# First MLP layer of chunks 2 to 5 by seven products over both halves, with staging in the MLP's tile and unpadded keys

## The chip, the cores and the metric

The kernel runs on one core of one Trainium2 chip. The metric is the device time of one execution in microseconds; for each kernel the median of several runs is given. Everything is computed in 32-bit floating point.

## The reference, cut to what matters

A delta-rule attention over B = 4 batches, H = 8 heads, S = 768 tokens and D = 48, followed by an MLP over all 3072 tokens, which see the eight heads side by side (384 features):

```
k_n = k / (norm(k) + 1e-6)
for t in range(S):
    y[t]  = q[t] @ state
    v_old = k_n[t] @ state
    state = state + beta[t] * outer(k_n[t], v[t] - v_old)
x = y, tokens in rows, 384 features
h = x @ w_in              # 384 -> 2048
out = (h * sigmoid(h)) @ w_out   # 2048 -> 384
```

## The kernel before, in words

The attention is computed in six chunks (NCH) of 128 tokens (C), each in two halves of 64 (W). All 32 pairs of batch and head go together, in two groups g of two batches. Within a half, the recurrence is solved with the inverse of a triangular 64x64 matrix per head. For a chunk c the steps are:

- **Scores** (`prepare`, `score`, line 550). Keys and queries are needed with D on the partitions. For chunks 0, 1 and the keys of 2 `turn` (line 514) transposes them on TensorE, with four 128x128 transposes into one bank. From then on `load_blocks` (line 151) fetches them by DMA in blocks of 32 into `stage`, and `turn_blocks` (line 504) transposes these on VectorE (DVE) with the 32x32 stream transpose of line 509. The products of keys with keys and queries leave PSUM through ScalarE and through `mask` on DVE (line 560). `block_out` and `block_in` send the key blocks through DRAM into another layout, g ("g<-blocks").
- **Inverse** (`invert`). 31 steps of a rank-one update on DVE, each a pair of operations (lines 648 and 653), and a last one (656); a copy of g (568); the results go through DRAM again ("low", "up", "xe").
- **Solve** (`solve`), a generator of nine steps: `merge` (801) twice, `keys` (843: state times keys, and the subtraction from v at line 852), `inner` (854, evacuated as z), `old` (923), `update` (872: the products pu, and their addition to the state at line 886) and `new` (935). The output of the attention, `pyc`, becomes `xT`, the transposed input of the MLP, by copies and DMAs.

The MLP of chunk c has two halves of 256 tokens. `hidden(c, hf)` (line 1061) makes w_in products: for each of 8 f, two j and three blocks a of 128 input features one matmul 128x128x256, 48 for a half; each float32 matmul is two instructions in the trace. A Silu on ScalarE (1078) puts 128x512 into `gT`, a tile out of a pool of three. `combine(c, hf)` then does the second layer by seven products instead of eight of block matrices (line 1175, chains of eight matmuls with 192 columns), with sums of g made on DVE by `sum_g` (1157) and sums of w_out made once.

The order of every engine's instructions is written out by hand (`pin`). For chunks 0 and 1 a script text gives it; from the end of chunk 1 a loop does. The MLP of the chunk before is cut into pieces by `yield`; `run(n)` puts n pieces at that place in the order of TensorE (and of the engines that evacuate). So the MLP's pieces lie between the steps of the attention. A piece of `hidden` is three or so matmuls, one of `combine` four. Almost all DMAs are issued from SP's queue, one after another in program order.

Where the loop of chunk c stood, before: nine steps of solve(c) with pieces between them, two steps of prepare(c + 1) with two pieces each, the scores, eight pieces, the 31 steps of the inversion with three pieces to four steps, and ten pieces with the squares and norms of chunk c + 2's keys (`lengths`).

## Time and profile before

| | us |
|---|---|
| median of three runs | 638.84 (637.5 to 639.85) |
| span of the profiled execution | 643.2 |
| busy in it: TensorE (PE) | 626.0 |
| VectorE (DVE) | 398.6 |
| ScalarE (ACT) | 216.7 |
| GpSimd (POOL) | 93.7 |

The profile is of one execution and is a little longer than the median of the runs. PE is TensorE's matmul unit, PEld its load of weights, which lies beside matmuls. An engine's busy time over the span says how much of the time it worked, not whether something waited for it; that is read from the chain of work that ended last, from timelines and from windows of the trace. Durations of single matmuls in the groups are latencies and overlap; the rate is read from stretches of the chain.

### The profile page before, as it was taken

How to read it: one execution, taken by the hardware profiler on the slowest of the kernel's cores; microseconds unless marked ns; L12 is line 12 of the kernel's file. 1: busy time of each engine (PE TensorE's matmuls, PEld its weight loads, DVE VectorE, ACT ScalarE, POOL GpSimd, SP SyncE). 2: the span in 40 equal slices, each digit the busy share in tenths (PEclk: the TensorE clock that was granted, in tenths of full speed). 3: DMA queues.
4: the chain of work that ended last, by engine and by line, in shares of the span. 5: the costliest groups of instructions: out<-in, count | busy, mean ns of one | idle time of the engine just before them, and what ended most of it. 6: DMA issues, size and time to landing. Idle time of an engine off the chain costs nothing.

```text
span 643.2 us, 21887 instructions
## 1 busy us (share of the span) xinstructions
PE 626.0 (97%) x9650; PEld 550.3 (86%) x9650; DVE 398.6 (62%) x902; ACT 216.7 (34%) x510; POOL 93.7 (15%) x95
## 2 busy tenths in 40 slices
PE   7889999999999999999999999999999999999997
PEld 5677778666689988999989999989989989889997
DVE  5853788998765985563986563987565974212112
ACT  3554756142342122452122451122451122441120
POOL 5422721246010020010020010020001000000000
PEclk9858999999999999999999999999999999999999
DMA  7755554170369333368433268334173033100101
GB/s 153 176 111 175 189 117 112 50 148 4 85 129 153 56 90 38 61 131 143 57 87 47 52 132 145 63 83 52 36 146 75 12 78 46 40 14 1 25 0 25
DMA packets 141694, 53.68 MB, mean 83 GB/s; under 512 B 113296, under 2 KB 135056, under 8 KB 141600
## 3 DMA queue, kind: packets, MB, share of 16 engines
q1 hardware_dynamic: 141120, 51.62, 39.6%
q8 instruction: 76, 1.25, 0.9%
q10 hardware_dynamic: 480, 0.67, 0.4%
q14 instruction: 18, 0.15, 0.1%
HBM read 39.62 MB, written 10.49 MB: 78 GB/s over the span
## 4 chain that ended last, share of the span: by engine, by line
PE 94%; DVE 3%; issue 2%; DMA 1%; SPq 0%; ACT 0%; POOL 0%; DVEq 0%; POOLq 0%
PE phid L1068 40%; PE px L1175 16%; PE py L1175 12%; PE po L1103 7%; PE pa L550 3%; PE pz L859 2%; PE ph L847 2%; PE pyc L940 2%; PE pu L879 2%; PE pyc L927 1%; PE pt L521 1%; PE px L801 1%; PE py L801 1%; PE pw L349 1%; PE pl L752 1%
## 5 line engine op out<-in xcount | busy, mean ns | idle before, releaser
L1068 PE MATMUL phid<-xT,w_in 128*128 128x256 f32 x1152 | 259.4, 383 | 0.2
L1068 PEld LDWEIGHTS phid<-xT,w_in 128*128 128x128 f32 x1152 | 216.8, 191 | 31.7 <-issue 2.1
L1078 ACT ACTIVATE gT<-phid 128x512 f32<-128x512 f32 x88 | 52.5, 597 | 146.0 <-PE phid L1068 138.8
L648 DVE SCALAR_TENSOR_TENSOR rank<-g,step,x 128x31 f32<-128x31 f32 (+15 forms) x124 | 49.8, 401 | 37.4 <-DMA g<-blocks 34.0
L1157 DVE TENSOR_TENSOR sums_of_g<-gT 128x384 f32<-128x384 f32 (+1 forms) x60 | 30.6, 530 | 55.4 <-ACT gT L1078 44.8
L1175 PE MATMUL py<-w_out,sums_of_g 128*128 128x192 f32 x320 | 56.8, 329 | 0.0
L1175 PE MATMUL px<-sums_of_w,sums_of_g 128*128 128x192 f32 x320 | 56.6, 329 | 0.0
L1175 PEld LDWEIGHTS px<-sums_of_w,sums_of_g 128*128 128x128 f32 x320 | 52.2, 190 | 0.5
L1175 PEld LDWEIGHTS py<-w_out,sums_of_g 128*128 128x128 f32 x320 | 52.2, 190 | 0.4
L653 DVE TENSOR_TENSOR x<-x,rank 128x31 f32<-128x31 f32 (+15 forms) x124 | 42.5, 343 | 4.3
L488 POOL TENSOR_TENSOR vf<-vf,n_slot 128x768 f32<-128x768 f32 x10 | 14.7, 1478 | 168.2 <-DMA vf<-in_v_dram 93.0
L886 DVE TENSOR_TENSOR state<-state,pu 48x384 f32<-48x384 f32 x44 | 24.3, 552 | 23.2 <-PE pu L879 22.3
L565 ACT COPY xT<-pyc 48x128 f32<-48x128 f32 (+2 forms) x120 | 31.1, 259 | 1.6
L509 DVE STREAM_TRANSPOSE kq<-stage 128x512 f32<-128x512 f32 x28 | 28.0, 1101 | 3.6 <-DMA stage<-in_q_dram 3.1
L1175 PE MATMUL px<-sums_of_w,gT 128*128 128x192 f32 x160 | 28.4, 329 | 0.0
L1175 PE MATMUL py<-w_out,gT 128*128 128x192 f32 x160 | 28.4, 329 | 0.0
L1175 PE MATMUL px<-w_out,gT 128*128 128x192 f32 x160 | 28.0, 327 | 0.0
L859 PEld LDWEIGHTS pz<-vf,xi 64*64 64x64 f32 x768 | 25.1, 142 | 3.2 <-issue 2.6
L571 POOL COPY g<-x 64x256 f32<-64x256 f32 x4 | 5.0, 1242 | 155.4 <-DVE x L656 155.4
L1175 PEld LDWEIGHTS px<-w_out,gT 128*128 128x128 f32 x160 | 26.4, 190 | 0.5
L859 PE MATMUL pz<-vf,xi 64*64 64x48 f32 x768 | 26.7, 226 | 0.0
L1175 PEld LDWEIGHTS py<-w_out,gT 128*128 128x128 f32 x160 | 26.1, 190 | 0.3
(202 smaller groups left out, 833.7 us busy)
## 6 DMA issues: line engine op xcount, KB each, us to landing
vf<-in_v_dram SPq DMA_DIRECT2D x48, 96.0 KB, 3.3
out_dram<-o SPq DMA_DIRECT2D x42, 96.0 KB, 2.2
w_out<-in_moe_w_in_dram SPq DMA_DIRECT2D x12, 256.0 KB, 3.3
sums_of_w<-in_moe_w_out_dram SPq DMA_DIRECT2D x8, 384.0 KB, 3.9
blocks<-ap SPq DMA_DIRECT2D x40, 64.0 KB, 1.9
kb<-in_k_dram SPq DMA_DIRECT2D x12, 192.0 KB, 4.4
kb<-in_k_dram SPq DMA_DIRECT2D x24, 96.0 KB, 4.5
raw<-in_moe_w_in_dram SPq DMA_DIRECT2D x9, 256.0 KB, 3.8
```

Of the source, the lines that this page charges most:

```text
L509: pin(nc.vector.transpose(out=kqs[c, b][:, :, j, :].rearrange("p a (i m) -> p a m i", i=T), in_=src.rearrange("p a (m d) -> p a m d", d=D) ...
L550: pin(nc.tensor.matmul(pa[e][half, p * n * W : (p + 1) * n * W], lhsT=kq[rows, p, 0, half], rhs=kq[rows, p, js[0] : js[-1] + 1, half], sta ...
L565: return pin(nc.scalar.copy(to, of))
L648: pin(nc.vector.scalar_tensor_tensor(out=tv, in0=g[:, 0:m, m : m + 1].to_broadcast([P, m, n]), scalar=step[:, m : m + 1], in1=x[:, m : m + ...
L653: yield pin(nc.vector.tensor_tensor(out=x[:, 0:m, m:T], in0=x[:, 0:m, m:T], in1=tv, op=ALU.add))
L859: yield pin(nc.tensor.matmul(pz[rows, n * D : (n + 1) * D], lhsT=xis[g][rows, u * H + 2 * p + e, :], rhs=vfs[c][rows, hf, g * HB + u, p, : ...
L886: pin(nc.vector.tensor_tensor(out=to, in0=to, in1=by_heads(pu[of]), op=ALU.add))
L1068: pin(nc.tensor.matmul(ph[:, j * GT : (j + 1) * GT], lhsT=w_in[:, a, (2 * f + j) * P : (2 * f + j + 1) * P], rhs=xTs[c, hf][:, a, :], star ...
L1078: pin(nc.scalar.activation(out=hidden_of(c, hf, f), in_=ph[:], func=ACTF.Silu, scale=-0.5 if in_blocks(c) else 0.5))
L1103: pin(nc.tensor.matmul(pos[i][:, 0:DM], lhsT=hidden_of(0, hf, f // 2)[:, at : at + C], rhs=w_outs[f // HFF][:, f % HFF, :], start=(f == 0) ...
L1157: pin(nc.vector.tensor_tensor(out=sums_of_g[:, k, fs], in0=of[0], in1=of[1], op=op))
L1175: pin(nc.tensor.matmul(to, lhsT=at, rhs=quarter(f, *b) if isinstance(b, tuple) else sums_of_w[b][:, f], start=start and f == 0, stop=f == ...
```

## The change

- **Hidden layer by products of blocks.** For chunks 2 to 5 `hidden_by_products` takes both halves, `early` and `late`, together. Two of the three input blocks (a = 0 and 1), the two halves of the tokens and the two column sets j make a 2x2 by 2x2 product of blocks, computed by seven products; the third block stays plain. Per chunk these are 44 items of two matmuls of 128x128x256. Needed for it: sums of w_in in `wS` (`sum_w_in`, eight operations on DVE, once), differences of x per chunk (`sum_x`, five on DVE), and parts that are put into gT by ScalarE (`keep`) and added to there from PSUM by DVE (`add`, 12 of 128x512 per chunk). It takes one bank from each of the pools A and CC and two of pool M during its 44 items.
- **Staging.** `stage` is gone; the blocks of k and q are loaded into parts of gT (one constant tile now), of `ap0s` (single now) and of wS. Keys, z and queries lie unpadded, so that `turn` uses eight matmuls of 128x64 by the identity in place of four transposes.
- **Order.** The loads of q group 0 stand after the first merge, those of group 1 behind the transposes of k's group 0; q's transposes stand in the solve, ahead of `made` (update and new) of the second half. The scores of c + 1 follow the solve after one piece; the loads of v follow the round trip of the blocks; the inversion has one piece with each step. A cycle consumes 72 pieces where it was some 60. `combine` goes over f in another order and keeps one `kept` part.

The diff, cut to its core:

```diff
...
-    kbufs = [const.tile([P, B, NP, 2, W], FP32, name=f"kb{s}") for s in range(2)]
-    zbuf = const.tile([P, B, 2, NP, W], FP32, name="z")
+    ROW = HB * H * D
+    PADDED = ROW + W - D
+    kbufs = [const.tile([P, 2, PADDED], FP32, name=f"kb{s}") for s in range(2)]
+    zbuf = const.tile([P, 2, PADDED], FP32, name="z")
...
+    gT = const.tile([P, 2, NFF // 2, 2 * GT], FP32, name="gT")
+    wS = const.tile([P, 3, NFF // 2, C], FP32, name="sums_of_w_in")
+    halves = [gT[:, i].rearrange("p f t -> p (f t)") for i in range(2)]
+    spare_s = wS[:].rearrange("p k f t -> p (k f t)")
+    ap0s = const.tile([P, 2, HB, H, W], FP32, name="ap0")
+    runs = {}
+    def run_room(c, j):
+        half = halves[int(c == 3)]
+        for g in range(2):
+            at = 0
+            if c == 2:
+                of, at = spare_s, HB * NP * RUN * g
+            elif j == 0:
+                of, at = half, HB * NP * RUN * g
+            else:
+                of = ap0s[:].rearrange("p g u h t -> p (g u h t)") if g == 0 else half
+            runs[c, j, g] = of[:, at : at + HB * NP * RUN].rearrange("p (n r) -> p n r", r=RUN)
...
-        src, kq = (kbufs[c % 2], queries[c] if c < 2 else None)[j][:, b], kqs[c, b]
+        src, kq = (kbufs[c % 2], queries[c] if c < 2 else None)[j], kqs[c, b]
         pt = bank(room, "pt")
         for p in range(NP):
-            pin(nc.tensor.transpose(
-                pt[:, p * C : (p + 1) * C], src[:, p].rearrange("p e w -> p (e w)"), ident[:]
-            ))
+            for e in range(2):
+                pin(nc.tensor.matmul(
+                    pt[W * e : W * (e + 1), p * C : (p + 1) * C], lhsT=wide(src, b, p, e), rhs=ident[:],
+                    start=True, stop=True,
+                ))
...
-                aps[c, g][j] = work.tile([P, HB, H, W], FP32, name=f"ap{j}", tag=f"ap{j}", bufs=2)
+                aps[c, g][j] = ap0s[:, g] if j == 0 else work.tile([P, HB, H, W], FP32, name="ap1", tag="ap1", bufs=2)
...
-            load_blocks(q, c + 1, slice(HB * g, HB * (g + 1)))
+            if c == 1 or g == 1:
+                load_blocks(q, c + 1, slice(HB * g, HB * (g + 1)))
...
+        if c > 1 and in_blocks(c + 1):
+            load_blocks(q, c + 1, slice(0, HB))
...
-            if hf == 1:
-                if c == 1:
-                    follow(c)
+            if hf == 1 and c == 1:
+                follow(c)
                 load_v(c + 1)
+            elif hf == 1 and in_blocks(c + 1):
+                for b in range(B):
+                    turn_blocks(c + 1, b, 1)
...
+    sums_of_x = sums_of_g[:, 0].rearrange("p f t -> p (f t)").rearrange("p (i t) -> p i t", t=GT)
+    def w_of(a, j):
+        return w_in[:, a].rearrange("p (f j t) -> p f j t", j=2, t=P)[:, :, j]
+    def sum_w_in():
+        n = NFF // 4
+        for to, left, right, op in (
+            (wS[:, 0], w_of(0, 1), w_of(1, 1), ALU.add), (wS[:, 1], wS[:, 0], w_of(0, 0), ALU.subtract),
+            (wS[:, 2], w_of(1, 0), wS[:, 1], ALU.subtract), (w_of(0, 1), w_of(0, 0), w_of(0, 1), ALU.subtract),
+        ):
+            for i in range(2):
+                fs = slice(n * i, n * (i + 1))
+                yield pin(nc.vector.tensor_tensor(out=to[:, fs], in0=left[:, fs], in1=right[:, fs], op=op))
+    UNITS = (3, 0, 1, 2)
+    def sum_x(c):
+        early, late = (xTs[c, hf] for hf in range(2))
+        for to, left, right in (
+            (sums_of_x[:, 0], late[:, 0], early[:, 0]), (sums_of_x[:, 1], late[:, 1], sums_of_x[:, 0]),
+            (late[:, 0], late[:, 1], late[:, 0]), (sums_of_x[:, 2], early[:, 1], sums_of_x[:, 1]),
+            (sums_of_x[:, 3], early[:, 2], late[:, 2]),
+        ):
+            pin(nc.vector.tensor_tensor(out=to, in0=left, in1=right, op=ALU.subtract))
+    def hidden_by_products(c):
+        rooms = [A.popleft(), CC.popleft()]
+        held = [bank(M, "hu") for _ in range(2)]
+        outer = [banks.tile([P, 512], FP32, name="hx", tag=tag) for tag in rooms]
+        early, late = (xTs[c, hf] for hf in range(2))
+        scale = -0.5
+        def product(to, weights, moving, fs, start=False):
+            for i, f in enumerate(fs):
+                pin(nc.tensor.matmul(
+                    to[:, GT * i : GT * (i + 1)], lhsT=weights[:, f], rhs=moving,
+                    start=start and i == 0, stop=True, skip_group_check=True,
+                ))
+        def at(fs, j, hf):
+            return gT[:, hf, fs[0] : fs[0] + 2, GT * j : GT * (j + 1)]
+        def of(held):
+            return held[:].rearrange("p (f t) -> p f t", f=2)
+        def keep(room, fs, j, hf):
+            return lambda: by_act(at(fs, j, hf), of(room))
+        def add(room, fs, j, hf):
+            return lambda: pin(nc.vector.tensor_tensor(
+                out=at(fs, j, hf), in0=at(fs, j, hf), in1=of(room), op=ALU.add
+            ))
+        def silu(fs, j, hf, room=None):
+            to = at(fs, j, hf)
+            return lambda: pin(nc.scalar.activation(
+                out=to, in_=to if room is None else of(room), func=ACTF.Silu, scale=scale
+            ))
+        def both(fs):
+            to = gT[:, 1, fs[0] : fs[0] + 2, :]
+            return lambda: pin(nc.scalar.activation(out=to, in_=to, func=ACTF.Silu, scale=scale))
+        items = []
+        for k in range(2):
+            a, b = ((2 * u, 2 * u + 1) for u in UNITS[2 * k : 2 * k + 2])
+            ua, ub = held
+            xa, xb = outer
+            items += [
+                (xa, w_of(1, 0), early[:, 1], a, True, None),
+                (ua, w_of(0, 0), early[:, 0], a, True, keep(ua, a, 0, 0)),
+                (xa, w_of(2, 0), early[:, 2], a, False, add(xa, a, 0, 0)),
+                (xb, w_of(1, 0), early[:, 1], b, True, None),
+                (ub, w_of(0, 0), early[:, 0], b, True, keep(ub, b, 0, 0)),
+                (xb, w_of(2, 0), early[:, 2], b, False, add(xb, b, 0, 0)),
+                (xa, wS[:, 0], sums_of_x[:, 0], a, True, (silu(a, 0, 0), keep(xa, a, 1, 1))),
+                (ua, wS[:, 1], sums_of_x[:, 1], a, False, keep(ua, a, 0, 1)),
+                (ub, wS[:, 1], sums_of_x[:, 1], b, False, keep(ub, b, 0, 1)),
+                (xb, wS[:, 0], sums_of_x[:, 0], b, True, (silu(b, 0, 0), keep(xb, b, 1, 1))),
+                (xa, wS[:, 2], late[:, 1], a, False, None),
+                (xa, w_of(2, 0), late[:, 2], a, False, add(xa, a, 0, 1)),
+                (ua, w_of(0, 1), late[:, 0], a, False, None),
+                (ua, w_of(2, 1), late[:, 2], a, False, add(ua, a, 1, 1)),
+                (ub, w_of(0, 1), late[:, 0], b, False, both(a)),
+                (ub, w_of(2, 1), late[:, 2], b, False, add(ub, b, 1, 1)),
+                (xb, wS[:, 2], late[:, 1], b, False, None),
+                (xb, w_of(2, 0), late[:, 2], b, False, add(xb, b, 0, 1)),
+                (ua, w_of(1, 1), sums_of_x[:, 2], a, False, both(b)),
+                (ua, w_of(2, 1), sums_of_x[:, 3], a, False, silu(a, 1, 0, ua)),
+                (ub, w_of(1, 1), sums_of_x[:, 2], b, False, None),
+                (ub, w_of(2, 1), sums_of_x[:, 3], b, False, silu(b, 1, 0, ub)),
+            ]
+        waiting = ()
+        for n, (to, weights, moving, fs, start, after) in enumerate(items):
+            if n == 0:
+                sum_x(c)
+            product(to, weights, moving, fs, start)
+            for one in waiting:
+                one()
+            waiting = () if after is None else after if isinstance(after, tuple) else (after,)
+            if n == len(items) - 1:
+                for one in waiting:
+                    one()
+                A.append(rooms[0])
+                CC.append(rooms[1])
             yield
...
-    def feed_forward(c, hf):
-
-        yield from hidden(c, hf)
-        yield from combine(c, hf)
+    def feed_forward(c):
+        if c > 1:
+            yield from hidden_by_products(c)
+        for hf in range(2):
+            if c == 1:
+                yield from hidden(c, hf)
+            yield from combine(c, hf)
...
-            for g in range(2):
-                size(c, g)
             if c == 2:
+                for g in range(2):
+                    size(c, g)
                 yield
                 for b in range(B):
                     turn(c, b, 0, (A, CC)[b % 2], True)
-            for g in range(2):
-                for b in range(HB * g, HB * (g + 1)):
-                    turn_blocks(c, b, 1)
-                yield
+                for g in range(2):
+                    for b in range(HB * g, HB * (g + 1)):
+                        turn_blocks(c, b, 1)
+                    yield
             for b in range(B):
                 scored(b)
...
-    for c in range(1, NCH):
-        if c > 1:
-            solving = solve(c)
-            for n in range(9):
-                go(solving)
-                run(((2, 2, 2, 2, 1, 1, 2, 2, 2), (2, 2, 2, 1, 1, 2, 2, 2, 2))[c == NCH - 1][n])
-                if n == 5:
-                    pieces = chained(pieces, feed_forward(c, 0), feed_forward(c, 1))
+    assert next(solving, 0) == 0
+    go(long_2, 99)
+    ready = prepare(2)
+    for _ in range(3):
+        go(ready)
+        run(1)
+    step = block_steps(2)
+    go(ready)
+    run(6)
+    for n, _ in enumerate(invert(2, step)):
+        run(int(n % 4 != 3 and n != 24))
+        if n == 3:
+            load_k(3)
+        if n == 24:
+            load_blocks(k, 3, ALL)
+    after, sums_in = lengths(3), sum_w_in()
+    for n in range(6):
+        go(after, 5)
+        go(sums_in)
+        run()
+    go(after, 99)
+    for c in range(2, NCH):
+        solving = solve(c)
+        for n in range(8):
+            go(solving)
+            run((2, 2, 2, 2, 1, 1, 2, 2)[n])
+            if n == 1 and c > 2 and c + 1 < NCH:
+                load_blocks(k, c + 1, ALL)
+            if n == 5 and c == 2:
+                go(sums_in, 2)
+        go(solving)
+        run()
         assert next(solving, 0) == 0
-        go(long_2, 99)
-        if c + 1 < NCH:
-            ready = prepare(c + 1)
-            for _ in range(3 if c == 1 else 2):
-                go(ready)
-                run(2)
-            step = block_steps(c + 1)
-            go(ready)
-            run(8 if c > 1 else 6)
-            for n, _ in enumerate(invert(c + 1, step)):
-                run(int(n % 4 != 3 and n != 24))
-                if n == 3:
-                    load_k(c + 2)
-                    if in_blocks(c + 2):
-                        load_blocks(k, c + 2, ALL)
-            after = lengths(c + 2) if c + 2 < NCH else iter(())
-            for _ in range({1: 8, NCH - 2: 10}.get(c, 10)):
-                run()
-                go(after, 4)
-            go(after, 99)
+        if c == 2:
+            pieces = chained(pieces, *(feed_forward(c) for c in range(2, NCH)))
+        if c + 1 == NCH:
+            break
+        step = block_steps(c + 1)
+        ready = prepare(c + 1)
+        go(ready)
+        load_v(c + 1)
+        run(5)
+        for g in range(2):
+            size(c + 1, g)
+        run(7)
+        for n, _ in enumerate(invert(c + 1, step)):
+            run()
+            if n == 3:
+                load_k(c + 2)
+        after = lengths(c + 2) if c + 2 < NCH else iter(())
+        for _ in range(13):
+            run()
+            go(after, 3)
+        go(after, 99)
     run(999)
```

132 lines of the change are left out of this document (75 added, 57 removed).

## The prediction

> **What bounds the kernel now.** I read the page first: the busy line and the chain of work that ended last.
>
> ```profile
> span 643.2 us, 21887 instructions
> PE 626.0 (97%) x9650; PEld 550.3 (86%) x9650; DVE 398.6 (62%) x902; ACT 216.7 (34%) x510; POOL 93.7 (15%) x95
> PE 94%; DVE 3%; issue 2%; DMA 1%; SPq 0%; ACT 0%; POOL 0%; DVEq 0%; POOLq 0%
> ```
>
> TensorE (PE) is the bound: busy 97%, and 94% of the chain. The page's execution spans 643.2 us, 4.4 more than the median of 638.84 (637.5 to 639.85); I take differences from the trace and add them to the median. Next come the windows of the trace, cut where one chunk's cycle ends and the next begins (chunks 2, 3, 4; columns PE, PEld, DVE, ACT, POOL busy, clock, DMA).
>
> ```profile
> 221.10:317.80 96.70, 96.00 (x1443) 88.28 (x1443) 63.09 (x151) 29.15 (x75) 8.43 (x9) 1.00 0.50 88
> 317.80:413.40 95.60, 95.60 (x1444) 88.11 (x1443) 62.33 (x149) 29.27 (x75) 8.48 (x9) 1.00 0.48 89
> 413.40:509.20 95.80, 95.80 (x1443) 88.19 (x1442) 65.75 (x152) 29.17 (x76) 8.50 (x9) 1.00 0.33 66
> ```
>
> From chunk 2 on PE has no idle time at all and a granted clock of 1.00. A matmul less is therefore worth its whole length, and a new wait costs its whole length as well: there is no slack to swallow it. VectorE (DVE) is at 62 of 95.6 us, so it has room on average, not at each place.
>
> **What is removed.** The chain of waits, one cycle's stretches:
>
> ```profile
> 264.28 1.08 PE ph L847 x64
> 265.36 2.80 PE px L1175 x16
> 270.16 2.80 PE py L1175 x16
> 272.96 0.86 PE pu L879 x64
> 273.82 0.90 PE pyc L940 x64
> 274.72 7.97 PE phid L1068 x36
> 282.69 0.14 PE pg L466 x2
> 282.83 3.65 PE pa L550 x128
> ...
> 317.83 20.72 PE phid L1068 x96
> ```
>
> The last row is one half's hidden stage: 48 matmuls, two instructions each, so 0.216 us per instruction and 0.432 per matmul. A chunk has 96 of them and gets 88; four chunks save 32 x 0.432 = **13.8 us**. One new item (two matmuls) lasts 0.863 us.
>
> **What is added to PE: the transposes.** A turn (line 521) was four 128x128 transposes; it becomes eight matmuls of 64x128 output, 16 instructions.
>
> ```profile
> 182.91 1.75 PE pt L521 x16
> L521 PE MATMUL pt<-ident,kb 128*128 128x128 f32 x48 | 7.0, 288 | 0.0
> ```
>
> Four turns took 1.75 us, 0.44 each. A 128-column instruction is half of 0.216, 0.108 us. The score's (pa L550, 128 columns) took 3.65/128 = 0.0285 us each in four tiles, so different tiles run beside each other. With two column tiles side by side a turn costs 16 x 0.054 = 0.86, 0.42 more; one after another 1.73, 1.29 more. There are 20 turns (eight each in chunks 0 and 1, four in chunk 2); of these I count 15 on the path, the others standing beside waits for the weights. That is 15 x 0.42 = **+6.3 us** (0 to 19). The Trainium skill, TensorEngine Tiling (Array Packing), section Tiling Modes, lists 128x64 as two independent tiles, which is the side-by-side case; no run here shows that mode on 128 rows.
>
> **Stall A, at the score (chunks 3, 4, 5, so three times).** Before, 7.97 us of hidden matmuls stood between the last state product and the score. Now the score (line 586) follows after one piece, and all transposes of q have moved ahead of the state updates on DVE. The timeline of DVE there (start, busy, line, and in brackets the idle time before it):
>
> ```profile
> 265.41 1.02 DVE L852 TENSOR_TENSOR vf<-vf,ph 128x384 f32<-128x384 f32 x2 [1.08 <-PE ph L847]
> 266.35 3.94 DVE L509 STREAM_TRANSPOSE kq<-stage 128x512 f32<-128x512 f32 x4
> ...
> 273.90 2.30 DVE L886 TENSOR_TENSOR state<-state,pu 48x384 f32<-48x384 f32 x4
> 276.23 2.04 DVE L509 STREAM_TRANSPOSE kq<-stage 128x512 f32<-128x512 f32 x2
> 278.76 2.04 DVE L509 STREAM_TRANSPOSE kq<-stage 128x512 f32<-128x512 f32 x2 [0.49 <-issue]
> 284.32 3.38 DVE L560 TENSOR_TENSOR ap<-pa,above 128x256 f32<-128x256 f32 x8 [3.51 <-ACT ap L565]
> ```
>
> Count from the end of ph as zero. PE would reach the score after 2.80 + 2.0 (pz and pyc, 268.16 to 270.16) + 2.80 + 0.86 + 0.90 + 1.4 (one MLP piece, half of 2.80) + 0.2 (pg and the change of tiles) = 11.0 us and end it 3.65 later, at 14.6. DVE's order is now: vf to 1.07, k transposes to about 5, one or two MLP adds of 0.55 each, q group 0 (2.04) to about 8. Then q group 1 must have landed. Its room is that of the k blocks of group 0, so its DMAs can be issued only after the second k transpose, about 3.05. Timeline of SP's queue, and the table of DMA issues of the same stretch:
>
> ```profile
> 268.41 6.35 SPq L160 DMA_DIRECT2D stage<-in_q_dram  x12
> stage<-in_q_dram SPq DMA_DIRECT2D x4, 88.0 KB, 4.6
> ```
>
> Twelve issues in 6.35 us make 3.2 for six; with 4.6 of landing behind the last one's start the data are there at about 10.1. Transposes to 12.1, two adds 1.2, state updates 2.3, to about 15.5; then the masks (3.38/8 = 0.42 each). The score's second and third groups need the banks that the state updates read, and its fourth needs the first's masks, done at about 16.5. The score ends at about 17.4 instead of 14.6: **2.85 us each time**, 8.6 in all (1.8 if the transfer lands early, 3.2 if a us later). This is a new wait behind which all PE work queues; on DVE the state updates and masks queue behind the landing.
>
> **Stalls B and C, in the hidden stage beside the inversion (three times).** The groups of the whole trace, then of 299.5 to 331.65, then the timeline. The products need 12 additions into gT per chunk on DVE, out of PSUM, 128x512, and five differences of x.
>
> ```profile
> L560 DVE TENSOR_TENSOR ap<-pa,above 128x256 f32<-128x256 f32 x40 | 15.0, 419 | 11.6 <-ACT ap L565 10.2
> L852 DVE TENSOR_TENSOR vf<-vf,ph 128x384 f32<-128x384 f32 x22 | 11.3, 551 | 13.1 <-PE ph L847 10.4 <-POOL vf L488 2.6
> L648 DVE SCALAR_TENSOR_TENSOR rank<-g,step,x 128x31 f32<-128x31 f32 (+15 forms) x31 | 12.4, 401 | 11.7 <-DMA g<-blocks 10.8
> L653 DVE TENSOR_TENSOR x<-x,rank 128x31 f32<-128x31 f32 (+15 forms) x31 | 10.6, 343 | 1.1
> 329.51 1.22 DVE L656 TENSOR_TENSOR x<-x,step 128x1024 f32<-128x1024 f32 x1
> 330.77 0.84 DVE L568 COPY g<-x 64x768 f32<-64x768 f32 x1
> ```
>
> 0.419 at 256 columns and 0.551 at 384 extrapolate to 0.68 at 512; in the stream the neighbours overlap a little, so 0.5 net. The inversion's 31 pairs are 12.4 + 10.6 busy and, with 0.03 between operations, 25 us. After the score come four left-over pieces of the MLP, then items 0 to 43; the inversion's steps stand beside items 8 to 39. There PE has 32 x 0.863 = 27.6 us and DVE 25 + 9 x 0.5 = 29.5 (31.1 at 0.68). DVE is the bound of this stretch, and PE stands still where an item needs the bank that a late addition has not read: **B = 1.6 us** (0 if additions hide in the gaps, 3.5 at 0.68). Then the twelfth addition is queued behind L656 and the copy of g: pairs end about 1 us after item 39, then 1.22 + 0.84 + 0.5. The activation of both (1024 columns) and one silu follow.
>
> ```profile
> L1078 ACT ACTIVATE gT<-phid 128x512 f32<-128x512 f32 x88 | 52.5, 597 | 146.0 <-PE phid L1068 138.8 <-DVE rank L648 4.1 <-DVE sums_of_g L1157 2.0
> ```
>
> 0.597 at 512 columns; I take 1.03 at 1024. So the bank of the output product is free 1 + 2.6 + 1.03 + 0.6 = 5.2 us after item 39, while items 40 to 43 fill 3.45: **C = 1.8 us** (0 to 2.5). B + C make 3 x 3.4 = 10.2. Chunk 5 has no inversion, DVE is free there, and the stage costs nothing. Before, the same 30-odd us of inversion stood beside output products and plain hidden matmuls, with the sums of g as DVE's only other work, and no PE instruction waited.
>
> **Once, in chunk 2:** its first merge comes two pieces earlier.
>
> ```profile
> 241.75 1.29 PE L801 MATMUL py<-xe,ap 32*32 32x32 f32 x128
> xe<-low SPq DMA_DIRECT2D x2, 128.0 KB, 2.2
> ```
>
> The chain and the DMA table of that place. I count a wait of **2.2 us** (0 to 4) for the round trip of xe, since PE had no wait there and two pieces are up to 5.2. The eight sums of w_in stand on DVE beside six pieces of PE work and are costed at nothing; without that cover their eight operations would be about 0.7 each.
>
> **The moved DMAs.** The eight loads of v, 0.77 us each, go behind the round trip of the score's blocks instead of ahead of it, and the 12 of k's blocks into the solve.
>
> ```profile
> 288.13 5.86 SPq L104 DMA_DIRECT2D blocks<-ap  x8
> 299.57 0.27 DVE L648 SCALAR_TENSOR_TENSOR rank<-g,step,x 128x31 f32<-128x31 f32 x1 [10.82 <-DMA g<-blocks]
> ```
>
> From the first block's issue to the first step of the inversion it was 11.4 us. In the new order the first block is issued about 1 us before the score ends, so the step can start 10.4 after it, and it is due behind four pieces (5.2) and eight items (6.9), at 12.1. I cost these moves at nothing; with the 1.7 us of cover gone, each us late on SP is a us of B.
>
> **Sum:** -13.8 + 6.3 + 8.6 + 10.2 + 2.2 = +13.5; 638.8 + 13.5 = **652 us**.
>
> **The rivals.** *Faster:* DVE keeps up. Per cycle it gains 12 x 0.68 + 5 x 0.42 = 10.3 us, 72 to 76 of some 92: that speaks for it; the dense stretch beside the inversion speaks against it. A to C and the merge vanish: 638.8 - 13.8 + 6.3 = 631. *Parity:* A at its lower bound 1.8, B nothing, C 0.75: 3 x 2.55 = 7.7, so 639. *Clock:* the wait A lowers PE's clock; windows of the trace (columns as above):
>
> ```profile
> 31.00:34.00 3.00, 2.70 (x128) 2.56 (x128) 1.07 (x3) 1.63 (x3) 2.24 (x2) 0.50 0.53 105
> 34.00:38.00 4.00, 2.53 (x127) 2.39 (x126) 2.92 (x6) 2.83 (x8) 0.25 (x1) 0.50 0.65 123
> 176.00:182.00 6.00, 4.93 (x142) 4.11 (x141) 2.42 (x6) 2.11 (x6) 0.00 (x0) 1.00 0.84 175
> ```
>
> At 31 to 38 us a stretch with 25% idle ran at 0.50; at 176, with 1.07 us idle, at 1.00. A's 2.85 us lies between; it decides when one gap passes about 2 us. Seven us at half rate cost 3.5, three times 10.5: 663. The Trainium skill, TensorE: Matmul & The Clock Gate, Part 1, has the clock halve after a whole idle window of about 3.4 us; by that a gap of 2.85 would not do it, and the stretch at 31 us, with 2.70 busy of 3, does not look like such a window. *Serial transposes:* 15 x 0.87 = 13 more, 665. That 88 matmuls are not what runs is excluded by the changed kernel's order of instructions.
>
> **Chances.** The forecast 0.51 (its own range 645 to 660), faster 0.18, parity 0.16, clock 0.09, serial 0.06. What a measurement can tell is about 0.5%, 3.2 us. Faster by more takes the first rival and a little of parity, 0.20; slower takes the forecast, clock and serial, 0.64. The range 633 to 664 leaves out some 0.12 below and 0.07 above.
>
> **What would show it.** In the changed profile: 704 matmul instructions of the products; cycles of 98.6 us (95.8 - 3.45 + 2.85 + 3.4) instead of 95.8; PE idle ahead of line 586 put down to DVE's state update or mask; idle ahead of line 1166 put down to the addition on DVE, line 1181; idle ahead of line 1330 put down to ACT, line 1187; a turn of 0.86 us; a merge of chunk 2 waiting for xe. A cycle of 92 us (95.8 less 3.45) without idle PE would make the prediction wrong by the first rival; windows below 1.00 would show the third.

## The result, and the profile after

The changed kernel takes 671.94 us (median of six runs, 669.46 to 675.09) against 639.04 (637.5 to 640.74) for the kernel before: a ratio of 1.0517, 95% interval 1.0483 to 1.0552. It is 33 us slower. The forecast was 652, with a range that ended at 664: the direction was right, the size was not.

The page of the profile after:

```profile
span 673.3 us, 22364 instructions
PE 637.4 (95%) x9826; PEld 556.7 (83%) x9826; DVE 436.2 (65%) x943; ACT 240.5 (36%) x542; POOL 93.0 (14%) x95
PEclk9669999999999989979999969999999999999999
PE 67%; DVE 19%; issue 5%; ACT 3%; DMA 3%; SPq 2%; POOL 0%; DVEq 0%; POOLq 0%; ACTq 0%
```

PE was 94% of the chain of work that ended last and is 67% now; DVE is 19%. PE is busy 11 us longer although 32 matmuls are gone, and it stands still 19 us longer. The row of the clock has new dips in its slices 15, 18 and 24 (of 16.8 us each), where it read 9 before. What PE waited for, from 200 us to the end (in all, how often, longest):

```profile
PE pa L586 <- ACT xT L601: 6.4, 6, 1.2
PE py L838 <- DMA xe<-low: 5.8, 2, 5.5
PE px L1330 <- ACT gT L1187: 4.7, 3, 1.6
PE hx L1166 <- DVE gT L1181: 4.4, 6, 1.1
```

The four lines are the score, the first merge of chunk 2, the output products behind the hidden stage and the items of the hidden stage. In the kernel before there is no such line in this stretch of more than 0.4 us. Two cycles, from score to score, and the places where the clock fell (columns as in the prediction: length, busy PE, PEld, DVE, ACT, POOL, clock, DMA):

```profile
287.40:390.10 102.70, 96.97 (x1429) 87.94 (x1429) 74.38 (x163) 34.98 (x84) 8.43 (x9) 0.97 0.39 82
390.10:493.30 103.20, 98.20 (x1428) 89.58 (x1428) 72.08 (x161) 34.97 (x84) 8.43 (x9) 0.95 0.39 82
248.00:256.00 8.00, 5.60 (x138) 4.85 (x139) 7.67 (x24) 1.75 (x3) 0.00 (x0) 0.57 0.99 151
288.00:290.00 2.00, 1.11 (x29) 0.87 (x25) 1.94 (x5) 1.93 (x8) 0.00 (x0) 0.80 0.13 35
290.00:296.00 6.00, 6.00 (x98) 5.67 (x91) 3.87 (x11) 2.03 (x7) 1.10 (x2) 0.50 0.32 58
391.60:401.80 10.20, 9.72 (x110) 9.39 (x111) 4.39 (x11) 3.09 (x11) 1.11 (x2) 0.50 0.35 61
494.00:500.00 6.00, 5.11 (x124) 4.69 (x117) 4.93 (x12) 3.87 (x14) 1.11 (x2) 1.00 0.33 63
595.30:633.40 38.10, 38.10 (x178) 33.55 (x178) 10.38 (x18) 15.18 (x24) 0.00 (x0) 1.00 0.04 11
```

And the same two cycles of the kernel before:

```profile
282.80:379.60 96.80, 96.80 (x1451) 89.16 (x1451) 63.64 (x151) 29.67 (x76) 7.65 (x9) 1.00 0.47 84
379.60:476.70 97.10, 97.10 (x1453) 89.35 (x1452) 63.42 (x151) 29.34 (x76) 8.47 (x9) 1.00 0.47 87
```

A cycle has grown by 6 us. In the first, 102.70 - 96.97 = 5.7 us are idle; the 96.97 busy us stand against 96.80 - 3.45 = 93.4 that the work would need, so 3.6 us went to slower work, and the rows at 288 and 290 show it: 6 us at half rate lose 3.0, the 2 us before it 0.2. Behind the next score 10.2 us ran at 0.50 (half of 9.72 busy us, 4.9, lost); behind the third, at 494, none. The last row is chunk 5's hidden stage, with no inversion beside it: 44 items in 38.10 us without a wait, where two halves took 2 x 20.72. The saving is real.

Where the wait at the score comes from: PE, then ACT at the first of these scores.

```profile
287.38 1.10 PE L586 MATMUL pa<-kq 48*64 48x128 f32 x32 [1.23 <-ACT xT L601]
289.38 5.61 PE L586 MATMUL pa<-kq 48*64 48x128 f32 x96 [0.89 <-ACT xT L601]
```

```profile
284.63 1.06 ACT L601 COPY part<-pyc 48x512 f32<-48x512 f32 x2 [2.81 <-PE pyc L977]
285.72 1.62 ACT L601 COPY xT<-pyc 48x128 f32<-48x128 f32 x6
287.36 0.33 ACT L1338 ACTIVATE kept<-py 128x192 f32<-128x192 f32 x1
287.71 1.61 ACT L601 COPY xT<-pyc 48x128 f32<-48x128 f32 x6
```

The score's two PSUM banks hold the attention's outputs until ACT has copied them, in its own order: PE goes on at 287.38, when the first six copies end at 287.34, and at 289.38, when the second six end at 289.32. Before, PE had 7.97 us of hidden matmuls to do while these copies ran.

### The profile page after: what moved, and what is told of

The parts are those of the page before. It is cut to its first block, busy times and chain, and to the rows that moved or that the text cites. A ratio compares the mean times of both kernels' runs of the same rounds, so it can differ in the third digit from the quotient of the medians.

```text
span 673.3 us, 22364 instructions
## 1 busy us (share of the span) xinstructions
PE 637.4 (95%) x9826; PEld 556.7 (83%) x9826; DVE 436.2 (65%) x943; ACT 240.5 (36%) x542; POOL 93.0 (14%) x95
## 4 chain that ended last, share of the span: by engine, by line
PE 67%; DVE 19%; issue 5%; ACT 3%; DMA 3%; SPq 2%; POOL 0%; DVEq 0%; POOLq 0%; ACTq 0%
PE px L1330 14%; PE py L1330 10%; PE phid L1112 8%; DVE rank L684 7%; PE po L1256 6%; DVE x L689 6%; PE hx L1166 5%; PE hu L1166 4%; PE pa L586 4%; PE pt L556 3%; DVE gT L1181 3%; PE pz L896 2%; PE ph L884 2%; PE pw L383 2%; PE pyc L964 1%
## 5 line engine op out<-in xcount | busy, mean ns | idle before, releaser
L1112 PE MATMUL phid<-xT,w_in 128*128 128x256 f32 x384 | 90.4, 389 | 0.0
L1112 PEld LDWEIGHTS phid<-xT,w_in 128*128 128x128 f32 x384 | 71.8, 192 | 10.9 <-issue 0.7
L1166 PE MATMUL hx<-xT,w_in 128*128 128x256 f32 x192 | 48.0, 379 | 0.0
L1166 PE MATMUL hu<-xT,w_in 128*128 128x256 f32 x192 | 45.6, 380 | 0.5 <-ACT gT L1187 0.4
L1166 PEld LDWEIGHTS hu<-xT,w_in 128*128 128x128 f32 x192 | 36.3, 190 | 6.2 <-ACT gT L1187 1.3
L1310 DVE TENSOR_TENSOR sums_of_g<-gT 128x512 f32<-128x512 f32 (+2 forms) x44 | 26.3, 634 | 21.7 <-PE py L1330 16.1
L1166 PEld LDWEIGHTS hx<-xT,w_in 128*128 128x128 f32 x192 | 36.4, 190 | 4.8
L1181 DVE TENSOR_TENSOR gT<-gT,hx 128x512 f32<-128x512 f32 x32 | 21.9, 684 | 27.3 <-PE hx L1166 26.9
L586 PE MATMUL pa<-kq 48*64 48x128 f32 (+1 forms) x768 | 28.3, 306 | 8.4 <-ACT xT L601 6.4
L586 PEld LDWEIGHTS pa<-kq 48*64 48x64 f32 x768 | 24.9, 168 | 12.5 <-ACT xT L601 7.4
```

Source lines behind the costliest of these rows:

```text
L586: pin(nc.tensor.matmul(pa[e][half, p * n * W : (p + 1) * n * W], lhsT=kq[rows, p, 0, half], rhs=kq[rows, p, js[0] : js[-1] + 1, half], sta ...
L1112: pin(nc.tensor.matmul(ph[:, j * GT : (j + 1) * GT], lhsT=w_in[:, a, (2 * f + j) * P : (2 * f + j + 1) * P], rhs=xTs[c, hf][:, a, :], star ...
L1166: pin(nc.tensor.matmul(to[:, GT * i : GT * (i + 1)], lhsT=weights[:, f], rhs=moving, start=start and i == 0, stop=True, skip_group_check=True,
L1181: return lambda: pin(nc.vector.tensor_tensor(out=at(fs, j, hf), in0=at(fs, j, hf), in1=of(room), op=ALU.add))
L1310: pin(nc.vector.tensor_tensor(out=sums_of_g[:, k, fs], in0=of[0], in1=of[1], op=op))
```

## The experiments

Each was timed beside the kernel before on its own chip, and the times of that kernel there are given. What is compared between experiments is how far each lies behind that kernel (after: 32.9 us); a few us between chips mean nothing. "After" is the kernel after the change.

**one_ahead**, **four_ahead**: more pieces between the last state update and the score.

```diff
         go(solving)
-        run()
+        run(1 if c + 1 == NCH else 2)
...
-        for _ in range(13):
+        for _ in range(12):
```

That is one_ahead; four_ahead has 5 in place of 2, and 9 in place of 12.

> As the kernel after the change, but one more piece (1.3 us) ahead of each score of chunks 3 to 5, and one less behind the inversion. Theory: the idle time at the score falls from 2.1 to about 0.8 us, and no clock of 0.50 follows it any more: 4 + 10.6 us less, about 657. Rival (any gap before the small tiles of the score lowers the clock, whatever its length): windows of 0.50 remain behind two or three of the scores, 664 to 668.

Measured: 665.95 (before 642.22; ratio 1.0381, 1.0348 to 1.0415): 23.7 us behind, 9 less than after. The waits at the score are 0.89 us each, and the clock stays at 1.00 behind all three. The mechanism of the theory holds; the gain is smaller than forecast: the clock behind the scores cost some 8 us in the profiled execution of after (3.2 and 4.9), not 10.6, and that execution is the slowest of its six.

> In chunks 2 to 4 the four left-over pieces of the MLP stand ahead of the score instead of behind it and after the inversion nine pieces follow instead of thirteen; nothing else is changed. Theory (waits at the score plus the clock that they lower): the 2.1 us of idle PE at each score go (6.4 in all), the score and the pieces behind it run at a clock of 1.00 again (about 10.6 us), and the twelfth addition is no longer queued behind the inversion's end, so the wait of the output products (1.56 us, three times) goes too; together 22 us, about 650. Rival (the chain score, blocks, inversion, merge on DVE and the DMA queues sets the cycle): the waits only move to the items of the hidden stage and to the merge, the cycle stays over 100 us, and only the clock's share comes back: 660 or more.

Measured: 671.58 (before 642.22; ratio 1.0476, 1.0409 to 1.0543): 29.4 us behind, no gain clear of the noise. With four more pieces above it the first score waited longer, 2.35 us; the others waited 0.96 and 1.59. ACT again, at the first:

```profile
284.09 1.61 ACT L601 COPY xT<-pyc 48x128 f32<-48x128 f32 x6
285.73 0.33 ACT L1338 ACTIVATE kept<-py 128x192 f32<-128x192 f32 x1
290.12 0.33 ACT L1338 ACTIVATE kept<-px 128x192 f32<-128x192 f32 x1 [4.05 <-DVE o L1341]
291.13 0.33 ACT L1338 ACTIVATE kept<-py 128x192 f32<-128x192 f32 x1 [0.69 <-DVE o L1341]
291.49 1.61 ACT L601 COPY xT<-pyc 48x128 f32<-48x128 f32 x6
```

The moved pieces bring their own evacuations (kept) ahead of the second six copies. The second kept needs the only buffer, which DVE frees after the state updates; ACT stands for 4.05 us, and the score behind it. That is why neither theory fitted.

**copies_first**: the same four pieces, put behind the last step of the solve, so that ACT's copies come first.

```diff
         go(solving)
         run()
         assert next(solving, 0) == 0
...
+        run(4)
         step = block_steps(c + 1)
...
-        for _ in range(13):
+        for _ in range(9):
```

> As four_ahead, but the copies of the last attention output (six xT copies on ACT) are put ahead of the four pieces; in four_ahead they stood behind a second kept, which waits on ACT until DVE has added the first one. Theory (the score waits for ACT's evacuation, in program order): no idle PE at any score, no clock of 0.50 behind it, no wait of the output products; what is left of the loss is the turns, the merge of chunk 2 and about 1.3 us per cycle in the hidden stage: 672 - 6.4 - 6.5 - 4.7 = 654. Rival (DVE's order, with q's transposes ahead of the state updates, holds the score): idle of 1 us or more stays at each score, put down to the state update, 662 or more.

Measured: 664.18 (before 639.54; ratio 1.0402, 1.0344 to 1.0461): 24.6 us behind, 8 less than after, where 18 was expected. No wait at any score is left and the clock is 1.00 there; but the 6.4 us at the merge, 4.1 at the output products and 6.6 at the items of the hidden stage remain. The waiting engine is shown to be ACT. That C would go, because the last addition now stands ahead of the inversion's end, was wrong.

**no_second_op**: most of the inversion's second operation left out.

```diff
-                out=x[:, 0:m, m:T], in0=x[:, 0:m, m:T], in1=tv, op=ALU.add
+                out=x[:, 0:m, T - 1 : T], in0=x[:, 0:m, T - 1 : T], in1=tv[:, :, n - 1 : n], op=ALU.add
```

> As the kernel after the change, but the second operation of each step of the inversion updates one column only, so most of the inverse is left out; DVE has about 9 us less per cycle. Theory (the waits inside the hidden stage are DVE's queue): the idle time ahead of the items with line 1166 released by the additions goes, and the 1.56 us of the output products falls to under 0.7. Rival (the bank is free late because an addition can start only when its product ends): the waits stay at 1.1 and 0.45.

Measured in one run: 655.87 (before 639.54). Its waits from 200 us on:

```profile
PE pa L586 <- ACT xT L601: 6.4, 6, 1.2
PE py L838 <- DMA xe<-low: 2.7, 2, 2.0
PE pyc L977 <- issue: 0.2, 1, 0.2
```

The waits at the items (4.4) and at the output products (4.7) are gone altogether: both are DVE's queue, the additions behind the inversion's steps. The score's 6.4 are untouched by it.

**size_alone**: in after, POOL's multiplication of v by the steps (2.9 us) fell beside the inversion's first pair, and that pair took 1.25 and 1.42 us. Here it is moved.

```diff
             elif hf == 1 and in_blocks(c + 1):
+                load_v(c + 1)
...
         go(ready)
-        load_v(c + 1)
-        run(5)
         for g in range(2):
             size(c + 1, g)
-        run(7)
+        run(12)
```

> As the kernel after the change, but the loads of v are issued in the solve again, ahead of the score, and POOL's multiplication of v by the step sizes (2.9 us) stands right behind the score instead of five pieces later, where it lies beside the first pair of the inversion. Theory (that pair takes 1.25 and 1.42 us on DVE instead of 0.27 and 0.22 because of POOL's operation, and DVE's backlog of 2.2 us is what the items wait for): the pair takes 0.5 us together, the waits of 1.1 and 0.45 us ahead of the items of line 1166 go, and some of the 1.56 us at the output products: 6 to 8 us less than after, 665. Rival (the additions and the inversion together are too much for DVE in this stretch, whatever POOL does): these waits stay over 1 us per cycle, 670 to 672.

Measured: 669.59 (before 638.65; ratio 1.0488, 1.0435 to 1.0541). The pair is short again:

```profile
306.89 0.26 DVE L684 SCALAR_TENSOR_TENSOR rank<-g,step,x 128x31 f32<-128x31 f32 x1
307.19 0.21 DVE L689 TENSOR_TENSOR x<-x,rank 128x31 f32<-128x31 f32 x1
```

But the items wait 0.86 and 0.45 us instead of 1.11 and 0.45, and the output products 1.55 as before. The rival is right: with the short pair DVE stands idle for 1.45 us ahead of the next addition, so in after that idle time had absorbed most of the collision; the stretch behind it is too full by itself.

**loads_later** and **merge_pieces**: the first merge of chunk 2. In after, SP's queue held the start of the round trip:

```profile
236.70 6.90 SPq L196 DMA_DIRECT2D gT<-in_k_dram  x12
243.71 0.47 SPq L104 DMA_DIRECT2D low<-g  x1
247.71 0.92 SPq L708 DMA_DIRECT2D xe<-low  x2
```

g was ready at 242.2 (POOL's copy, 240.92 + 1.24), and low was issued at 243.71, behind the twelve loads.

```diff
-        if n == 24:
-            load_blocks(k, 3, ALL)
...
+    load_blocks(k, 3, ALL)
     after, sums_in = lengths(3), sum_w_in()
```

> As the kernel after the change, but the twelve loads of the k blocks of chunk 3 (6.9 us on SP's queue) are issued behind the round trip of the inverse of chunk 2 and not ahead of it. Theory (the first merge of chunk 2 waits for xe partly because low<-g is queued behind these loads): low is issued about 1.5 us earlier and the wait of 5.5 us falls to about 4; the clock of 0.50 behind it may stay; 669 to 671. Rival (the wait is the round trip itself and the pieces that no longer cover it, the queue does nothing): 672, the wait 5.5 as before.

Measured: 669.96 (before 642.22; ratio 1.0448, 1.0414 to 1.0483). The merge's wait fell from 5.8 to 3.8 us; the theory holds. Its three scores wait as in after, 1.23 and 0.89 us each, and this time the clock is 1.00 behind all three.

merge_pieces is copies_first with that move, and nine pieces instead of six ahead of the merge (one instead of four ahead of the score).

```diff
-    for n in range(6):
-        go(after, 5)
-        go(sums_in)
+    for n in range(9):
+        go(after, 4)
+        go(sums_in, int(n < 6))
```

> copies_first, and in chunk 2 the loads of k's blocks behind the round trip of the inverse, nine pieces instead of six ahead of the first merge, one instead of four ahead of the first score; the sums of w_in stay where they were. Theory (the wait for xe is PE running out of pieces, and the clock falls because of it): the wait of 6.4 us falls under 1, the stretch of 6 us at 0.50 behind it goes, about 9 us less than copies_first, 655. Rival (the round trip only starts later when the pieces move): 1 to 2 us less.

Measured: 661.07 (before 641.75; ratio 1.0305, 1.0256 to 1.0353). The wait for xe is gone, and so is the stretch at 0.50 behind it. Against copies_first it is 3 us in the medians (5 with the two chips' kernels before set against each other) where 9 was expected; its mean clock is 0.977 against 0.982 all the same, from longer stretches at 0.50 in the first 70 us, which the edit doesn't touch.

**copies_and_merge** was the same with the sums of w_in running on over all nine pieces; they then overwrite a part of w_in that chunk 1's MLP still needs.

> copies_first, and in chunk 2 the loads of k's blocks behind the round trip as in loads_later, and three more pieces ahead of the first merge (one instead of four ahead of the first score). Theory: the merge's wait of 5.5 us and the clock behind it go as well, 8 us less than copies_first: 646. Rival (the merge waits until the transfers end, wherever the pieces stand): 2 us less than copies_first.

Measured: 666.05 (before 639.54; ratio 1.0402, 1.0348 to 1.0456). The merge had no wait, but chunk 1's matmuls waited 8.8 us for DVE's sums of w_in. It tells nothing of the merge.

**both_last**: copies_first, and the silu that frees the output product's bank ahead of both.

```diff
-                (ua, w_of(1, 1), sums_of_x[:, 2], a, False, both(b)),
+                (ua, w_of(1, 1), sums_of_x[:, 2], a, False, None),
...
-                (ub, w_of(2, 1), sums_of_x[:, 3], b, False, silu(b, 1, 0, ub)),
+                (ub, w_of(2, 1), sums_of_x[:, 3], b, False, (silu(b, 1, 0, ub), both(b))),
```

> copies_first, with the last activation of 1024 columns of a chunk (both) issued on ACT behind the silu that frees the output product's bank instead of ahead of it. Theory (C: that silu is queued on ACT behind both, and both behind the twelfth addition on DVE): the wait of 1.36 us ahead of the output products goes in chunks 2 to 4, 4 us less than copies_first, 660. Rival (the bank or the sums of g are late anyway): the wait moves to the next chain, 663 to 664.

Measured: 662.97 (before 641.75; ratio 1.0335, 1.0267 to 1.0403): 21.2 us behind, against 24.6 for copies_first, with intervals that overlap. The wait at the output products is gone, and the wait of the items on DVE's additions rose from 3.9 to 6.4 us. So C's place in ACT's order was right, but the lag belongs to DVE, and it came back earlier in the same stage.

**turns_alone**: the kernel before, with only the transposes changed.

```diff
-            pin(nc.tensor.transpose(
-                pt[:, p * C : (p + 1) * C], src[:, p].rearrange("p e w -> p (e w)"), ident[:]
-            ))
+            for e in range(2):
+                pin(nc.tensor.matmul(
+                    pt[W * e : W * (e + 1), p * C : (p + 1) * C], lhsT=src[:, p, e, :], rhs=ident[:],
+                    start=True, stop=True,
+                ))
```

> The kernel before the change, with only the transposes changed: each turn is eight matmuls of 64x128 by the identity in place of four transposes. Theory: a turn costs 0.9 us instead of 0.44 with the two column tiles beside each other, and all twenty are on the path: 9 us more, 648. Rival (most turns of chunks 0 and 1 stand beside waits for weights): 2 to 4 us more, 641 to 643.

Measured: 653.58 (before 642.22; ratio 1.0192, 1.0128 to 1.0256): 11.4 us. Four turns of chunk 2, in the timeline of PE:

```profile
191.17 3.71 PE L522 MATMUL pt<-ident,kb 128*64 128x128 f32 x64
```

3.71/64 = 0.058 us per instruction, about half of 0.108, as two column tiles beside each other would give, and a turn takes 0.93 instead of 0.44. Twenty times 0.49 is 9.8, near the 11.4, but that all turns are on the path is not shown by it. In the profiled executions the whole loss lies ahead of the end of chunk 2's turns: the rest takes 458.65 us here and 458.54 in the kernel before. And of the 8.4 us that are lost ahead of chunk 2's turns (they start at 191.17 instead of 182.75), all are there after six of the sixteen early turns, at 32.35 instead of 23.98: with them come a wait of 2.13 us at 17.40 and a stretch at half rate from 17 to 31 us, of which the kernel before has only 20 to 23. The ten turns behind add nothing to the distance, but there the kernel before has half rate of its own, from 30 to 47 us. How much of the early loss is turns and how much the clock is open: four_ahead and after have the same early code, and chunk 2's turns start at 184.40 in the one, whose clock was 1.00 from 16 to 32 us, and at 188.63 in the other, where it was 0.51 and 0.64 in the two halves of that stretch.

**all_mended**, **mended_and_paced**, **paced_sums_later**: can the saving be had? all_mended joins copies_first, merge_pieces and both_last, gives bank xa two more items between its addition and its next use, and keeps the queries of chunks 0 and 1 padded, so that eight turns are four transposes again. The other two change the pace of the pieces:

```diff
         for n, _ in enumerate(invert(c + 1, step)):
-            run()
+            run(1 + int(n in (6, 9, 12, 15)) - int(n in (27, 29)))
...
-        for _ in range(9):
+        for _ in range(7):
```

That is mended_and_paced, which has size_alone's edit too; paced_sums_later leaves out the pieces of steps 30 and 31 as well and keeps nine behind.

> copies_first, both_last and merge_pieces together; the items of the hidden stage in an order that gives two more items between an addition and the next use of its bank xa; and the queries of chunks 0 and 1 padded again, so that eight of the twenty turns are four transposes. Theory: 664 less 4, less 9, less 1 to 2, less 8 x 0.5 for the turns: 646, still behind the kernel before by the twelve turns that are left (6 us) and what stays of the hidden stage's waits. Rival (the gain of 13 us of fewer products shows as soon as the waits are gone): 640 or less.

Measured: 650.89 (before 641.75; ratio 1.0113, 1.0037 to 1.0188). Left are 8.8 us of waits for DVE's additions, one of 2.28 us in each cycle, and 0.50 behind two of these.

> all_mended with the same move of v's loads and of POOL's multiplication, and with two more pieces beside the widest steps of the inversion (seven instead of nine behind it). Theory: the 2.28 us of idle PE per cycle and the stretches at 0.50 behind two of them (7 us) go: 651 - 14 = 637 to 640, the same as the kernel before. Rival (DVE's load as such): 1 us or more of idle PE per cycle stays and the time is 645 or more.

Measured: 652.22 (before 638.65; ratio 1.0201, 1.0170 to 1.0233). The waits at the items are gone, and the merges of chunks 3 to 5 wait instead, 7.1 us for xe. DVE behind the last step of the inversion (x<-x,rank; line numbers are this kernel's own):

```profile
323.86 0.19 DVE L700 TENSOR_TENSOR x<-x,rank 128x31 f32<-128x31 f32 x1
323.97 1.29 DVE L1322 TENSOR_TENSOR sums_of_g<-gT 128x512 f32<-128x512 f32 x2
325.18 1.29 DVE L1322 TENSOR_TENSOR sums_of_g<-sums_of_g,gT 128x512 f32<-128x512 f32 x2
326.38 1.22 DVE L703 TENSOR_TENSOR x<-x,step 128x1024 f32<-128x1024 f32 x1
```

The pieces had brought four sums of g ahead of the inversion's last operation, so the round trip began 2.4 us later.

> mended_and_paced, but no pieces stand beside the last two steps of the inversion (nine follow it instead of seven), so that the four sums of g (2.6 us on DVE) come behind the inversion's last operation and not ahead of it. Theory (the merge's waits of 2.4, 1.6 and 1.4 us for xe are those 2.6 us on DVE, at the start of the round trip): they go, 7 us less than mended_and_paced, 645, the kernel before or a per cent above it. Rival (the chain of scores, blocks, inversion and merge is as long as the cycle of PE, so a wait taken away at one place comes back at another): 1 us or more per cycle of idle PE, at the items, the output products or the merge, and 650 or more.

Measured: 644.82 (before 641.53; ratio 1.0052, 1.0020 to 1.0085). Its waits from 200 us on:

```profile
PE py L1342 <- DVE sums_of_g L1322: 4.1, 6, 1.8
PE pa L597 <- ACT xT L612: 0.5, 1, 0.5
```

The merge's wait is gone and 4.1 us are left at the sums of g. Both sides were partly right: each wait had its own cause, and each time a part of the lag of DVE came back at the next place. This version is about as fast as the kernel before, not faster: twelve turns of 0.93 us are left (12 x 0.49 = 5.9), with 4.6 us of waits. With the saving of 13.8 that would make it 3 us faster than the kernel before; some 6 us are not accounted for.

## Why the prediction was right or wrong

- **The saving** was right: 38.10 us for chunk 5's stage against 41.44, 3.3 for each chunk, and 13.8 was forecast for four.
- **The turns** were mis-sized: 6.3 was forecast, 11.4 measured (8 to 16 by the interval). 0.42 each was near (0.49). Whether the count of 15 of 20 on the path was wrong is open, since the early loss is in part waits and clock (turns_alone); the sum had neither. The Trainium skill, TensorEngine Tiling (Array Packing), section Tiling Modes, has two independent tiles at 128x64; the 0.058 us agree with it.
- **Stall A** had the right place and nearly the right size (2.85 forecast, 1.23 + 0.89 = 2.12 measured), by the wrong engine. The second group of q landed when forecast (DVE began on it at 285.33, and ph had ended at 275.16: 10.2 us, forecast 10.1); but PE waited for ACT's copies out of PSUM, and what I had put first, DVE's state update, is not among the waits at all. copies_first and four_ahead show it. That the size came near is luck.
- **Stall B** (1.6) and **C** (1.8) came as forecast: 1.56 and 1.57 in the first cycle. no_second_op shows that both are DVE's queue. What failed in C was the reason: not only the inversion's end stands ahead of the twelfth addition, since in copies_first, where it does not, 1.36 us remained.
- **The merge of chunk 2** was mis-sized: 2.2 forecast, 5.8 measured. I had counted two pieces less and had cost the loads of k's blocks in SP's queue at nothing. The queue was about 2 of the 5.8 us (loads_later), the missing pieces the rest (merge_pieces).
- **The clock** is the step that failed. I set it among the rivals, at 0.09, as another case, with a gap of 2.85 us too short to decide. It is a term that is added to the others, and the sum had it at nothing: two of three scores and the merge were followed by 7 to 10 us at 0.50 in the profiled execution, 2.4 (5.60 x 0.43) + 3.2 + 4.9 = 10.5 us. That the rival had the same 10.5 is luck; it was three equal losses at the scores and none at the merge. How the terms add up: -13.8 + 11.4 + 6.4 + 4.4 + 4.7 + 5.8 + 10.5 = 29.4 of 32.9. The 11.4 come from another kernel. Between the two profiled executions the difference is 30.1 us (673.3 - 643.2): 7.7 up to the end of chunk 2's turns (192.34 against 184.66) and 22.4 behind it, where -13.8 + 21.3 + 10.5 = 18.0 are named. Either way some 4 us stay unassigned.

What lowers the clock is not the length of a gap alone. Gaps of 0.89 us (one_ahead, three times) never did, nor those of 1.36 to 1.57 us ahead of the output products; 5.5 us and more at the merge always did. Single gaps of 2.28 us in all_mended did in two of three, and the pair of 1.23 and 0.89 us in five of twelve: twice in after, twice in no_second_op, once in size_alone, never in loads_later. The traces show what these five have in common. In each trace the clock changes only at steps of 3.41 us (a stretch at 0.50 lasts 3.4, 6.8, 10.2, 13.7 or 17.1 us), and the steps lie differently against the kernel in each execution. The steps around the three scores of after, with the columns as above:

```profile
285.77:289.18 3.41, 1.49 (x36) 1.14 (x34) 3.38 (x7) 3.25 (x13) 0.00 (x0) 1.00 0.14 36
388.17:391.58 3.41, 1.79 (x38) 1.43 (x36) 3.35 (x7) 3.23 (x13) 0.00 (x0) 1.00 0.12 34
490.57:493.98 3.41, 2.18 (x34) 2.07 (x37) 3.38 (x6) 3.27 (x11) 0.00 (x0) 1.00 0.11 29
493.98:497.39 3.41, 2.52 (x92) 2.28 (x88) 3.23 (x8) 2.67 (x11) 0.83 (x1) 1.00 0.12 34
```

Where one step holds most of the pair, PE is busy for 1.4 to 1.8 of its 3.41 us, and the next step runs at 0.50; that is so in all five. In the other seven the pair is divided between two steps, PE is busy for 2.0 us or more in each, and the clock stays. So with the same gaps it is chance where the steps fall. This is read from the traces; no run moves a gap on purpose. The Trainium skill, TensorE: Matmul & The Clock Gate, Part 1, has a window that runs freely of the kernel, by which it would depend on when the gap falls; the steps agree with that. That the whole window has to be idle, as the same part has it, does not agree: 1.6 us of idle PE in a step were enough. Its section on why this matters for kernels asks only that idle gaps stay under some 3 us. That disagrees with four_ahead, where one gap of 1.59 us, at 494, was followed by this:

```profile
492.00:496.00 4.00, 2.41 (x49) 2.12 (x51) 1.56 (x4) 2.44 (x10) 1.11 (x2) 1.00 0.07 16
496.00:498.00 2.00, 2.00 (x68) 2.00 (x67) 1.39 (x4) 1.16 (x4) 0.00 (x0) 0.83 0.65 157
498.00:504.00 6.00, 6.00 (x46) 4.86 (x39) 3.40 (x10) 1.75 (x5) 0.00 (x0) 0.50 0.55 94
```

The limit is not the same everywhere: 1.82 busy us in a step were enough to lower the clock at this score (493.92 to 497.33), and 1.82 were not beside the 128x128 matmuls of all_mended's second gap (409.28 to 412.69). Whether the small tiles of the score (48x64) count as less activity than full ones was not tried.

## What to carry to other kernels

When PE has no idle time, count for every removed piece of cover what each engine still has to do there in its own order, evacuations on ACT first, and add to each wait of 1.5 us or more the work that may run at half rate behind it: here 10.5 us beside 21 us of waits. Pieces that are moved bring their evacuations and sums into the queues of ACT and DVE; look at what they push back, not only at what they cover. A saving of 2% on the bound engine that puts 12 additions per chunk on an engine with a serial chain pays only if that chain has slack where they land.

## What the runs showed of the hardware that I had not expected

- PE's granted clock changed only at steps of 3.41 us that lie anew in each execution. The same pair of gaps, 1.23 and 0.89 us, was followed by 3.4 to 10.2 us at 0.50 when one step held most of it (five times), and by none when it was divided between two steps (seven times). A gap of 0.89 us alone never lowered the clock.
- While POOL multiplied v by the steps (2.9 us), two small DVE operations of 31 columns took 1.25 and 1.42 us instead of 0.26 and 0.21; with POOL's operation moved away (size_alone) they were short again.
- Matmuls of 64x128 with 128 rows take 0.058 us each in the stream, two column tiles together, against 0.109 for a 128x128 transpose, which is one instruction where the float32 matmul is two.
